# Moving ten of sixteen layernorm applications from VectorE to ScalarE, and rearranging the first ten microseconds of a fused attention and gated-MLP kernel

## The chip, the cores and the metric

The kernel runs on one core of one Trainium2 chip. The metric is device time in microseconds, lower is better. The profile of one execution comes with its own span, which is some 1.7 to 2.0 us shorter than the time on the metric, because it goes from the first to the last instruction.

Names used below: TensorE is PE in the profile, its weight loads are PEld, VectorE is DVE, ScalarE is ACT, GpSimd is POOL. SP is the engine that issues most DMAs; SPq and ACTq are the rows of DMA issues of SP and of ScalarE. PSUM is the memory that TensorE writes its results to; this kernel divides it into eight banks.

## The reference, cut to what matters

```python
x = A_x                                   # 1 x 2048 x 640, bf16
xn = layernorm(x)                         # (x - mean) / sqrt(var + 1e-5), per token
# branch A: 32 heads of 20, window of 8 positions at dilation 2
q, k, v = split(xn @ wqkv)
logits[s, w] = q[s] . k[s - 2*w] * 20**-0.5      # masked before the start
attn = softmax(logits, over w);  o[s] = sum_w attn[s, w] * v[s - 2*w]
# branch B: bilinear MLP, 640 -> 1536 -> 640
h = (xn @ w_gate) * (xn @ w_up)
out = x + o @ wo + h @ w_down
```

Of the kernel before, what the change touches and what calls it, by code (L numbers as in the profile page):

```python
# [5 lines left out]
ACT = mybir.ActivationFunctionType  # L6
ALU = mybir.AluOpType
# [3 lines left out]
NCH = 5  # L11
# [13 lines left out]
DHALF = D // 2  # L25
# [23 lines left out]
class Sched:  # L49
# [76 lines left out]
    def op(self, eng, fn, r=(), w=(), dma=False, name="", occ=None, lat=None, lock=False, nbytes=0, mode=0, group=None, extra=0.0):  # L126
        X = _Op()
        X.eng, X.fn, X.name, X.dma, X.group = eng, fn, name, dma, group
        X.needs_tick, X.event, X.pre_know, X.idx = False, None, None, len(self.ops)
        X.nth = self.n_eng[eng]  # L130
        self.n_eng[eng] += 1
        rk = [k for a in r for k in self.keys(a)]
        wk = [k for a in w for k in self.keys(a)]
        deps = self.deps_of(eng, rk, wk)
        if occ is None and not dma:
            occ = 0.1
        inorder = eng in ("pe", "act", "dve")
        start = max([self.t[eng]] + [d.end for d in deps.values()])
        if lock:
            start = max(start, self.t_lock)  # L140
        if eng == "pe" and mode != self.pe_mode:
            start += 0.1
            self.pe_mode = mode
        if dma:
            self.t[eng] = start + (0.48 if occ is None else occ)
            self.t_data = max(self.t_data, start + 1.2) + nbytes / 280e3
            X.end = self.t_data + 0.8 + extra
        else:
            self.t[eng] = start + occ
            X.end = start + (occ if lat is None else lat)  # L150
        if lock:
            self.t_lock = start + occ
        last = {}
        keep = []
        for d in deps.values():
            if d.dma or d.eng == "pool":
                keep.append(d)
            else:
                b = last.get(d.eng)
                if b is None or b.idx < d.idx:  # L160
                    last[d.eng] = d
        X.deps = keep + list(last.values())
        for d in X.deps:
            if not d.dma:
                d.needs_tick = True
        for k in rk:
            st = self.state.get(k)
            if st is None:
                self.state[k] = [None, [X]]
            elif inorder and st[1] and st[1][-1].eng == eng and not st[1][-1].dma:  # L170
                st[1][-1] = X
            else:
                st[1].append(X)
        for k in wk:
            self.state[k] = [X, []]
        if dma:
            if group is None or group not in self.groups:
                sem = self.nc.alloc_semaphore(f"dma{self.n_dma}")
                self.n_dma += 1
                if group is not None:  # L180
                    self.groups[group] = [sem, []]
            if group is None:
                X.event = (sem, 16)
            else:
                g = self.groups[group]
                g[1].append(X)
                X.event = (g[0], 16)
        self.ops.append(X)
        return X
# [151 lines left out]
def build_kernel(nc, A_x, A_wqkv, A_wo, B_x, B_w_gate, B_w_up, B_w_down, out):  # L341
    K = Sched(nc)
    op = K.op
# [3 lines left out]
    def sb(name, shape, dtype=BF16, at=None):  # L347
        n = mybir.dt.size(dtype)
        for s in shape[1:]:
            n *= s  # L350
        n = (n + 63) // 64 * 64
        if at is None:
            at = place[0]
            place[0] += n
        assert at + n <= 229344, (name, at + n)
        return K.sbuf(name, shape, dtype, at)
# [53 lines left out]
    MV = sb("MV", [128, NT, 16], FP32)  # L410
    SD = sb("SD", [128, NT, 16], FP32)
    DUM = sb("DUM", [128, 16], FP32)
    ZERO = sb("ZERO", [128, JB])
    EPSC = sb("EPSC", [128, 16], FP32)
    IDENT = sb("IDENT", [128, 128])
# [2 lines left out]
    PS = nc.alloc_psum_tensor("PS", [128, 8, 512], FP32)  # L418
# [8 lines left out]
    def mark(*k):  # L427
        done.add(k)
# [4 lines left out]
    def have(*k):  # L433
        return lambda: k in done
# [7 lines left out]
    def dma(o, i, r=(), w=(), name="", eng="sp", group=None):  # L442
        n = mybir.dt.size(o.dtype)
        for s in o.shape:
            n *= s
        return op(eng, lambda e: e.dma_start(o, i), r=r, w=w, dma=True, name=name, nbytes=n, group=group)  # L446

    op("dve", lambda e: e.memset(ZERO[:], 0.0), w=[ZERO[:]], name="zero", occ=0.2)
    op("dve", lambda e: e.memset(EPSC[:], EPS), w=[EPSC[:]], name="epsc", occ=0.1)
# [3 lines left out]
       r=[IDENT[:]], w=[IDENT[:]], name="ident", occ=0.4)  # L453
# [3 lines left out]
       r=[G[:]], w=[G[:]], name="g1", occ=0.3)  # L457
    op("pool", lambda e: e.affine_select(G[:], G[:], pattern=[[-4, H]], compare_op=ALU.is_ge,
                                         fill=0.0, base=0, channel_multiplier=1),
       r=[G[:]], w=[G[:]], name="g2", occ=0.3)  # L460
    op("pool", lambda e: e.memset(KT[:, :, 0:PAD], 0.0), w=[KT[:, :, 0:PAD]], name="kpad", occ=0.3)

    def xslot(t):
        return t + 4 if t < 8 else t - 8

    def x_load(t, eng="sp"):
        dma(XST[:, xslot(t), :], xhbm[t * TS:(t + 1) * TS, :], w=[XST[:, xslot(t), :]], name=f"xld{t}", eng=eng)
        mark("x", t)
# [44 lines left out]
    def front(t):  # L513
        x, st = XST[:, xslot(t), :], STATS[:, t, 0:12]
        xs, mv = XNS[:, t % NXN, :], MV[:, t, 0:2]
        sd, rstd = SD[:, t, 0:1], SD[:, t, 1:2]
        p = 0.1 * t

        def stats():
            for i in range(2):  # L520
                o, a = st[:, 6 * i:6 * i + 6], x[:, i * DHALF:(i + 1) * DHALF]
                op("dve", (lambda o, a: lambda e: e.bn_stats(o, a))(o, a), r=[a], w=[("st", t, i)], name=f"bn{t}_{i}", occ=0.49)  # L522

        def aggr():
            op("dve", lambda e: e.bn_aggr(mv, st), r=[("st", t, 0), ("st", t, 1)], w=[("mv", t)], name=f"bnag{t}", occ=0.2)

        def sqrt():
            op("act", lambda e: e.activation(sd, mv[:, 1:2], ACT.Sqrt, bias=EPSC[:, 0:1]), r=[("mv", t), EPSC[:]],
               w=[("sd", t)], name=f"sd{t}", occ=0.25)

        def apply():
            op("dve", lambda e: e.reciprocal(rstd, sd), r=[("sd", t)], w=[("rstd", t)], name=f"rstd{t}", occ=0.16)
            op("dve", lambda e: e.tensor_scalar(xs, x, mv[:, 0:1], rstd, op0=ALU.subtract, op1=ALU.mult),
               r=[x, ("mv", t), ("rstd", t)], w=[xs], name=f"lnap{t}", occ=0.45)
            mark("apply", t)

        yield have("x", t)
        yield Task("dve", stats, r=[x], prio=p)
        yield Task("dve", aggr, r=[("st", t, 1)], prio=p)
        yield Task("act", sqrt, r=[("mv", t)], prio=p)  # L540
        if t >= NXN:
            yield have("xnt", t - NXN)
        yield Task("dve", apply, r=[("sd", t), x], w=[xs], prio=p)
        o = XNT[:, :, t * TS:(t + 1) * TS]
        if t < N_PE_T:
            hold = []

            def trans(b):
                tpv = PS[:, b, :].bitcast(BF16)[:, 0:NCH * 128].rearrange("p (c f) -> p c f", c=NCH)
                for c in range(NCH):  # L550
                    i, q = xs[:, c * 128:(c + 1) * 128], tpv[:, c, :]
                    op("pe", (lambda q, i: lambda e: e.transpose(q, i, IDENT[:]))(q, i), r=[i, IDENT[:]], w=[q],  # L552
                       name=f"tr{t}_{c}", occ=0.057, lat=0.2)
                hold.append((b, tpv))
                if t == 0:
                    warm(3)

            def copy():
                b, tpv = hold[0]
                X = op("dve", lambda e: e.tensor_copy(o, tpv), r=[tpv], w=[o], name=f"xntcp{t}", occ=0.49)  # L560
                K.free_bank(b, X)

            yield Task("pe", trans, r=[xs], prio=p, banks=1)
            yield Task("dve", copy, r=[PS[:, hold[0][0], :]], prio=p)
        else:
            def dmat():
                op("sp", lambda e: e.dma_start_transpose(o, xs), r=[xs], w=[o], dma=True, name=f"dtr{t}", nbytes=200e3, occ=1.25, extra=1.3)

            yield Task("sp", dmat, r=[xs], prio=1)
        mark("xnt", t)  # L570

    def warm(n):
        for _ in range(n):
            op("pe", lambda e: e.matmul(PS[:, 7, 0:QB], ZERO[:, 0:128], ZERO[:, 0:QB], start=True, stop=True),
               r=[ZERO[:]], w=[PS[:, 7, :]], name="warm", occ=0.2 if n > 3 else 0.12)

# [422 lines left out]
    stores = []  # L999
# [53 lines left out]
                K.spawn(fin_thread())  # L1053

    N_PE_T = 5
    FIRST = 9
    GU_KEEP = 3

    x_load(0)
    x_load(1)  # L1060
    wqkv_load(0, 0, 3)
    wqkv_load(0, 3, NCH)
# [1 line left out]
    wqkv_load(1)  # L1064
    x_load(3)
    K.t["act"] = 2.1
    warm(22)

    def misc():
        yield have("xnt", NT - 1)  # L1070
# [65 lines left out]
```

## The kernel before: the parts that the change and the argument touch

The kernel is a program that makes a program. Each piece of work is a `Task` with an engine, the data it waits for, and a priority (a smaller number goes first). At build time a list scheduler with its own table of costs picks, per engine, among the tasks that it thinks are ready, and so fixes one order of instructions for each engine. On the chip each engine then works through its list in that order; if the next instruction has to wait, what stands behind it waits too.

The front, once for each of 16 tiles of 128 tokens (`...` marks cuts):

```python
def front(t):
    ...
    p = 0.1 * t
    def apply():
        op("dve", lambda e: e.reciprocal(rstd, sd), ...)
        op("dve", lambda e: e.tensor_scalar(xs, x, mv[:, 0:1], rstd, op0=ALU.subtract, op1=ALU.mult), ...)
    yield have("x", t)
    yield Task("dve", stats, r=[x], prio=p)          # two bn_stats of 320 columns
    yield Task("dve", aggr, r=[st], prio=p)
    yield Task("act", sqrt, r=[mv], prio=p)
    yield Task("dve", apply, r=[sd, x], w=[xs], prio=p)
    ...                                              # transposed on TensorE (tiles 0 to 4) or by DMA, into XNT
...
x_load(0); x_load(1); wqkv_load(0, 0, 3); wqkv_load(0, 3, NCH); x_load(2); wqkv_load(1); x_load(3)
warm(22)                                             # 22 dummy matmuls, to raise TensorE's clock
```

After the front come the projections to Q, K and V. Products of Q and K (tile PRD) are made on VectorE and summed to logits on TensorE. The softmax is done in two halves of 1024 tokens, nearly all on VectorE. V makes a detour: it is evicted to VST, stored to DRAM scratch in four parts of 512 tokens, and read back with shifted rows as VX. This detour and the copies of the softmax's result share one DMA queue:

```python
def store_v(j):                                       # one part of V: 640 KB
    yield num(NCH, "v", j)                            # its five evictions are done
    def go():
        dma(dst, VST[:, j], ..., name=f"vst{j}")      # on the SP queue
    yield Task("sp", go, r=[VST[:, j]], prio=20)

# in softmax(x): the weights move to another layout, 16 DMAs of 32 KB in one task
def move():
    for a in range(4):
        for q in range(4):
            ...
            dma(d, src, ..., name=f"atx{x}_{a}{q}")   # ATX <- LOG, also on the SP queue
yield Task("sp", move, r=[L[:]], prio=4)

# in vx_loads(): only when every logits block has been issued (num(NJ, "lg")), 4 DMAs a unit
yield have("vst", j)
yield Task("sp", go, prio=8, r=[("vscr", j)])         # VX <- v_scratch
```

While the attention goes on, TensorE fills its time with the gate and up projections of the MLP, each a group of five matmuls of 512 columns that needs one bank.

## Time and profile before

| | before |
|---|---|
| time, median of 3 runs (range) | 272.57 us (272.36 to 272.59) |
| span of the profiled run | 270.8 us |
| TensorE busy, share of the span | 265.4 us, 98% |
| VectorE busy, share of the span | 224.9 us, 83% |

The page of the kernel before starts with its span and with the busy time of every engine (share of the span, then number of instructions):

```profile
span 270.8 us, 4489 instructions
...
PE 265.4 (98%) x1811; PEld 153.6 (57%) x1811; DVE 224.9 (83%) x286; ACT 93.2 (34%) x169; POOL 96.5 (36%) x57
...
PE 89%; DVE 5%; DMA 3%; issue 1%; SPq 1%; ACT 0%; DVEq 0%
```

TensorE is the bottleneck: only 5.4 us of the span are without a matmul. The last line is the page's part 4, the chain of work that ended last, divided by engine.

The table of windows gives busy time and number of instructions of each engine in a stretch. These are the end of the front, the stretch in which tiles 6 to 15 are normalised, and the stretch around the second softmax, all of the kernel before:

```profile
core 0: us, PE busy (x) PEld busy (x) DVE busy (x) ACT busy (x) POOL busy (x), PEclk, DMA share, GB/s
6.72:10.84 4.12, 3.19 (x51) 2.85 (x51) 2.77 (x10) 1.65 (x4) 0.00 (x0) 1.00 1.02 352
20.00:33.00 13.00, 13.00 (x107) 11.24 (x106) 10.33 (x34) 8.55 (x21) 0.00 (x0) 1.00 0.52 87
96.00:112.50 16.50, 16.39 (x105) 7.17 (x104) 15.12 (x16) 8.07 (x12) 3.26 (x1) 1.00 0.82 210
```

In the first stretch TensorE is idle for 0.93 of 4.12 us. In the second it is never idle, and in the third hardly, for 0.11 us.

TensorE's timeline of the front, kernel before (start, duration, what; in brackets how long it was idle before, and who ended that):

```profile
1.26 4.59 PE L574 MATMUL PS<-ZERO 128*128 128x256 bf16 x22 [1.26 <-DVE EPSC L449]
5.69 0.44 PE L552 MATMUL PS<-IDENT,XNS 128*128 128x128 bf16 x5
...
9.03 1.31 PE L590 MATMUL PS<-XNT,WQKV 128*128 128x128 bf16 x20 [0.72 <-DVE XNT L560]
...
10.84 1.37 PE L590 MATMUL PS<-XNT,WQKV 128*128 128x128 bf16 x21 [0.22 <-DMA WQKV<-in_A_wqkv_dram]
```

These are the 22 dummies, the transposes of tile 0, the first four chunks of Q of tile 1, and K of tile 0, which waited for the second third of the projection weights.

### The profile page before, as it was taken

What the parts mean: (1) busy time and instruction counts of PE and PEld (TensorE: products, weight loads), DVE (VectorE), ACT (ScalarE), POOL (GpSimd) and SP (SyncE); (2) the same over time, 40 slices, a digit from 0 to 9 for tenths busy, and PEclk for the clock granted to TensorE, in tenths of its full rate; (3) what the DMA queues carried; (4) which work ended last, traced back from release to release, by engine and by line L of the source; (5) the groups of instructions that cost most, each with busy time, mean ns of one, the idle gap of its engine ahead of it and who ended that gap; (6) DMA issues with size and microseconds to landing.
All of it is one profiled execution on the core that took longest, in us unless ns stands there. A gap on an engine that the chain in (4) does not pass through costs nothing.

```text
span 270.8 us, 4489 instructions
## 1 busy us (share of the span) xinstructions
PE 265.4 (98%) x1811; PEld 153.6 (57%) x1811; DVE 224.9 (83%) x286; ACT 93.2 (34%) x169; POOL 96.5 (36%) x57
## 2 busy tenths in 40 slices
PE   7899999999999999999999999999999999999995
PEld 5897965454444444444444577544676776444775
DVE  5777799999999989999999999889989998623221
ACT  2466676555753245222433400433201202242000
POOL 1000000000000004077756876677857996600000
PEclk9999999999999999999999999999999999999999
DMA  6965459702343999127723356633364531100101
GB/s 202 361 207 83 92 81 322 264 0 97 99 130 78 240 207 319 39 49 163 177 69 80 105 130 166 185 83 79 79 174 132 138 88 48 48 2 0 48 27 48
DMA packets 39571, 33.46 MB, mean 124 GB/s; under 512 B 15232, under 2 KB 38272, under 8 KB 39552
## 3 DMA queue, kind: packets, MB, share of 16 engines
q1 hardware_dynamic: 39408, 33.15, 45.7%
q8 instruction: 14, 0.23, 0.4%
q10 hardware_dynamic: 144, 0.04, 0.1%
q14 instruction: 5, 0.04, 0.1%
HBM read 25.07 MB, written 5.26 MB: 112 GB/s over the span
## 4 chain that ended last, share of the span: by engine, by line
PE 89%; DVE 5%; DMA 3%; issue 1%; SPq 1%; ACT 0%; DVEq 0%
PE PS L966 33%; PE PS L1024 27%; PE PS L590 23%; DMA WQKV<-in_A_wqkv_dram 3%; PE PS L733 3%; PE PS L925 2%; DVE SM L762 2%; DVE PV L879 1%; SPq L446 1%; DVE HT L975 1%; DVE RS L782 1%; DVE M L762 0%; DVE LOG L773 0%; ACT PS L864 0%; PE PS L552 0%
## 5 line engine op out<-in xcount | busy, mean ns | idle before, releaser
L884 POOL TENSOR_TENSOR SV<-PV 128x1024 bf16<-128x1024 f32 x40 | 94.8, 2380 | 86.9 <-DVE PV L879 86.7
L879 DVE TENSOR_TENSOR PV<-VX,PS 128x1024 f32<-128x1024 bf16 (+1 forms) x56 | 92.9, 1670 | 1.7 <-ACT PS L864 1.7
L590 PE MATMUL PS<-XNT,WQKV 128*128 128x512 bf16 (+2 forms) x480 | 66.7, 299 | 1.2 <-DVE XNT L560 1.0
L966 PE MATMUL PS<-XNT,WG 128*128 128x512 bf16 x240 | 59.7, 379 | 0.1
L966 PE MATMUL PS<-XNT,WU 128*128 128x512 bf16 x240 | 59.7, 379 | 0.0
L590 PEld LDWEIGHTS PS<-XNT,WQKV 128*128 128x128 bf16 x480 | 43.4, 113 | 24.0 <-DVE XNT L560 1.7
L715 DVE TENSOR_TENSOR PRD<-QT,KT 128x2048 bf16<-128x2048 bf16 x40 | 46.1, 1218 | 0.0
L1024 PE MATMUL PS<-WD,HT 128*128 128x320 bf16 (+1 forms) x300 | 43.2, 294 | 0.0
L966 PEld LDWEIGHTS PS<-XNT,WU 128*128 128x128 bf16 x240 | 23.2, 98 | 29.1 <-ACT HT L595 0.8
L966 PEld LDWEIGHTS PS<-XNT,WG 128*128 128x128 bf16 x240 | 23.3, 98 | 28.6 <-DVE HT L975 0.6
L595 ACT ACTIVATE HT<-PS 128x512 bf16<-128x512 f32 x36 | 21.5, 597 | 51.6 <-PE PS L966 51.6
L1024 PEld LDWEIGHTS PS<-WD,HT 128*128 128x128 bf16 x300 | 28.6, 98 | 11.6 <-issue 0.4
L975 DVE TENSOR_TENSOR HT<-HT,PS 128x512 bf16<-128x512 bf16 x36 | 23.9, 683 | 12.7 <-PE PS L966 12.7
L1035 DVE TENSOR_TENSOR FOUT<-PS,XR 128x320 bf16<-128x320 f32 (+1 forms) x33 | 15.8, 478 | 16.9 <-PE PS L1024 16.5
L1024 PE MATMUL PS<-WO,OT 128*128 128x320 bf16 (+1 forms) x165 | 27.1, 295 | 0.0
L934 ACT ACTIVATE OT<-PS 128x512 bf16<-128x512 f32 x20 | 10.5, 600 | 36.8 <-PE PS L925 36.8
L1024 PEld LDWEIGHTS PS<-WO,OT 128*128 128x128 bf16 x165 | 15.9, 98 | 5.9
L752 POOL MEMSET LOG<- 32x6 bf16 (+6 forms) x7 | 0.4, 95 | 51.5 <-ACT LOG L744 51.5
L595 ACT ACTIVATE QT<-PS 128x512 bf16<-128x512 f32 (+1 forms) x22 | 12.3, 558 | 9.6 <-PE PS L590 9.5
L522 DVE BATCH_NORM_STATS2 STATS<-XST 128x6 f32<-128x320 bf16 x32 | 13.9, 476 | 2.0 <-DMA XST<-in_A_x_dram 1.9
L595 ACT ACTIVATE KT<-PS 128x512 bf16<-128x512 f32 (+1 forms) x22 | 12.2, 556 | 8.1 <-PE PS L590 8.1
L595 ACT ACTIVATE VST<-PS 128x512 bf16<-128x512 f32 x20 | 11.7, 597 | 8.1 <-PE PS L590 8.1
(43 smaller groups left out, 128.3 us busy)
## 6 DMA issues: line engine op xcount, KB each, us to landing
VX<-v_scratch SPq DMA_DIRECT2D x80, 130.0 KB, 2.9
XST<-in_A_x_dram SPq DMA_DIRECT2D x16, 160.0 KB, 7.1
v_scratch<-VST SPq DMA_DIRECT2D x4, 640.0 KB, 4.1
XR<-in_A_x_dram SPq DMA_DIRECT2D x16, 160.0 KB, 2.9
out_dram<-FOUT SPq DMA_DIRECT2D x15, 160.0 KB, 2.4
WG<-in_B_w_gate_dram SPq DMA_DIRECT2D x1, 1920.0 KB, 8.4
WU<-in_B_w_up_dram SPq DMA_DIRECT2D x1, 1920.0 KB, 12.0
WD<-in_B_w_down_dram SPq DMA_DIRECT2D x1, 1920.0 KB, 8.9
```

The lines of the kernel that those rows point to most:

```text
L522: op("dve", (lambda o, a: lambda e: e.bn_stats(o, a))(o, a), r=[a], w=[("st", t, i)], name=f"bn{t}_{i}", occ=0.49)
L590: op("pe", (lambda o, l, x, c, first: lambda e: e.matmul(o, l, x, start=first, stop=(c == NCH - 1)))(o, l, x, c, first), r=[l, x], w=[o], ...
L595: X = op("act", (lambda o, i: lambda e: e.activation(o, i, ACT.Copy))(o, i), r=[i], w=[o], name=name, occ=0.12 + n * 0.9e-3)
L715: op("dve", lambda e: e.tensor_tensor(s[:], qb, kv, ALU.mult), r=[q, rk], w=[s[:]], name=f"prod{j}_{r}_{c}", occ=1.15, lock=True)
L733: op("pe", (lambda o, x, a, c: lambda e: e.matmul(o, G[:], x, start=(c == 0), stop=(c == NCH - 1), tile_position=(0, 32 * a)))(o, x, a, c) ...
L879: op("dve", lambda e: e.tensor_tensor(p, vw, a, ALU.mult), r=[vv] + rk, w=[p], name=f"pv{u}_{x}_{r0}", occ=0.09 + 1.1 * nr)
L884: X = op("pool", lambda e: e.tensor_tensor(o, p[:, :, 0, :], p[:, :, 1, :], ALU.add), r=[p[:]], w=[o], name=f"pva{u}_{x}", occ=2.36, lock= ...
L934: X = op("act", (lambda o, b: lambda e: e.activation(o, PS[:, b, :], ACT.Copy))(o, b), r=[PS[:, b, :]], w=[o], name=f"oev{u}", occ=0.58)
L966: op("pe", (lambda l, x, c: lambda e: e.matmul(PS[:, b, :], l, x, start=(c == 0), stop=(c == NCH - 1)))(l, x, c), r=[l, x], w=[PS[:, b, :] ...
L975: X = op("dve", lambda e: e.tensor_tensor(h, h, PS[:, hold[1], :], ALU.mult), r=[h, PS[:, hold[1], :]], w=[h], name=f"h{m}_{j}", occ=0.65)
L1024: op("pe", (lambda l, x, i: lambda e: e.matmul(dst, l, x, start=(i == 0), stop=(i == n - 1)))(l, x, i), r=[l, x], w=[PS[:, b, :]], name=f" ...
L1035: X = op("dve", lambda e: e.tensor_tensor(o, PS[:, b, 0:wid], xr, ALU.add), r=[PS[:, b, :], xr], w=[o], name=f"fin{t}_{nb}", occ=0.15 + wi ...
```

## The change

It wants to shorten the front and to relieve VectorE: the first statistics of tile 1 go into VectorE's wait for tile 0's square root; a small read touches the weights' memory early; 18 dummies take the place of 22; and the normalisation of tiles 6 to 15 is done by ScalarE, as rstd * x - mean * rstd. One more thing happens that no line of the diff says: with these costs and priorities the scheduler puts five matmuls of Q (the fifth chunk of tiles 0 and 1) ahead of K. A setting `N_DVE_C = 5` has no effect, as only tiles 0 to 4 are copied there, so it is cut here.

```diff
+    TCH = sb("TCH", [128, 32])
 ...
+        def recip():
+            op("dve", lambda e: e.reciprocal(rstd, sd), ...)
+            if t >= N_DVE_A:
+                op("dve", lambda e: e.tensor_scalar(nmr, mv[:, 0:1], rstd, -1.0, op0=ALU.mult, op1=ALU.mult), ..., occ=0.13)
         def apply():
-            op("dve", lambda e: e.reciprocal(rstd, sd), ...)
-            op("dve", lambda e: e.tensor_scalar(xs, x, mv[:, 0:1], rstd, op0=ALU.subtract, op1=ALU.mult), ..., occ=0.45)
+            if t < N_DVE_A:
+                op("dve", lambda e: e.tensor_scalar(xs, x, mv[:, 0:1], rstd, op0=ALU.subtract, op1=ALU.mult), ..., occ=0.45)
+            else:
+                op("act", lambda e: e.activation(xs, x, ACT.Identity, bias=nmr, scale=rstd), ..., occ=0.75)
 ...
-        yield Task("dve", stats, r=[x], prio=p)
+        if t == 1:
+            yield have("sd", 0)
+        for i in range(2):
+            yield Task("dve", lambda: stats(i), r=[x], prio=-1 if t == 1 and i == 0 else p)
         yield Task("dve", aggr, r=[("st", t, 1)], prio=p)
-        yield Task("act", sqrt, r=[("mv", t)], prio=p)
+        yield Task("act", sqrt, r=[("mv", t)], prio=p - 1)
+        yield Task("dve", recip, r=[("sd", t)], prio=p)
 ...
-        yield Task("dve", apply, r=[("sd", t), x], w=[xs], prio=p)
+        yield Task("dve" if t < N_DVE_A else "act", apply, r=[("rstd", t), x], w=[xs], prio=p)
 ...
+    N_DVE_A = 6
 ...
     x_load(0)
+    tch = A_wqkv.rearrange("(p r) n -> p r n", r=NCH)[:, 0, 0:32]
+    stores.append(dma(TCH[:], tch, w=[TCH[:]], name="touch", eng="act"))
 ...
-    warm(22)
+    warm(18)
```

## The prediction

> **What bounds the kernel.** TensorE: the page gives PE 265.4 us busy of 270.8 (98%). The table of windows shows it busy 5.20 of 6.72 us before the first projection, 3.19 of 4.12 in 6.72-10.84, then at most 0.12 us idle in any stretch up to 229 us; after the last matmul come 2.7 us of eviction and store. From 10.84 us on the stream is dense, so a change in the front wins only what it starts earlier. Timeline of the front: x landed 3.1, statistics 3.12-4.01, square root to 4.57, normalised 5.26, last dummy 5.58, transposes 5.69, Q of tile 0 at 6.72, Q of tile 1 at 9.03 (PE idle 0.72 before it), K at 10.84, on the second weight third, landed 10.79.
>
> **The change, part by part.**
> 1. Fewer dummies: one starts every 0.213 us while the clock is low, so the row ends near 5.1. Tile 0's transposes start when it is normalised (about 5.4): up to 0.28 us earlier.
> 2. Tile 1's first statistics (0.44 us) in VectorE's 0.36 us wait for the square root: tile 0 loses 0.1, tile 1's Q starts at about 8.75 for 9.03.
> 3. The instruction order also moves Q's fifth chunk of tiles 0 and 1 (5 matmuls of 256 columns, 0.55 us) ahead of K, into the wait for the weights. This is the real gain: K starts at about 10.8 in both, with 0.55 us more done.
> 4. Touching read: DMA moves 113 and 159 GB/s in 3.0-4.0 us, against 330-380 later, just as weight reads begin. If the touch cures that, weights land up to 0.5 us earlier, but TensorE is busy until about 10.75 anyway: at most 0.1 us.
> 5. Ten normalisations to ScalarE: VectorE loses 10 x 0.45 us and gains ten one-column operations of about 0.13. ScalarE gains an estimated 0.9 us each: the square root of one column (0.29), plus 639 x 0.833 ns, plus 93 ns for a second pointer operand (the Trainium skill, "ScalarE: Activation LUTs", What ACT_TABLE_LOAD costs; the trace's 1.90 us for 2048 columns agrees with the slope). ScalarE, 67% busy in 16.7-31 us, becomes nearly full and falls an estimated 2 us behind TensorE; eight PSUM banks should carry this. VectorE starts the products some 3 us earlier, but no TensorE wait hangs on that.
>
> **Sum.** -0.6 us in the front, +0.1 for the chance of a bank wait in 20-36 us. Predicted 272.1 us, 8 times in 10 in 271.2 to 273.0. Chances: faster by over 2% 0.01, within 2% 0.97, slower by over 2% 0.02.
>
> **What would show it.** Timeline: transposes near 5.4, Q of tile 1 near 8.75, five 256-column matmuls before K, K at 10.5-10.9, no PE gap over 0.2 us later. Normalisation on ACT near 900 ns; ACT near 95% busy in 20-33 us; no PE wait on ACT. About 300 GB/s in 3.0-4.0 us if the touch works.
>
> **What would make it wrong.** TensorE's clock rose at about 5.4 us (dummies 213 ns apart before, 110 after). The Trainium skill, "TensorE: Matmul & The Clock Gate", What's actually happening, gives a busy window of about 3.4 us; 18 dummies end before the rise, and if it then comes later, the first projection (20 matmuls, 56 ns apart) takes about 1 us longer. ScalarE could delay evictions until TensorE waits for banks, +1 us or more. Weights that land much earlier could make the order pay more.

## More of the kernel before

The SP queue between 68 and 96 us, kernel before. The duration spans all DMA issues of a row:

```profile
70.64 4.55 SPq L446 DMA_DIRECT2D v_scratch<-VST  x2
75.68 10.46 SPq L446 DMA_DIRECT2D ATX<-LOG  x16
86.18 0.59 SPq L446 DMA_DIRECT2D v_scratch<-VST  x1
86.89 8.25 SPq L446 DMA_DIRECT2D VX<-v_scratch  x16
```

Three of the four V stores are issued before the 16 copies of the attention weights (the first of them at 61.66), one after. Those 16 copies are small, but their issuing alone takes 10.46 us. The third store was issued at 74.83 and had landed at 78.52; the fourth landed at 91.77.

VectorE in the stretch around the second softmax, kernel before:

```profile
97.14 2.35 DVE L879 TENSOR_TENSOR PV<-VX,PS 128x1024 f32<-128x1024 bf16 x2 [1.16 <-ACT PS L864]
...
100.12 0.75 DVE L762 TENSOR_TENSOR M<-M 128x512 bf16<-128x512 bf16 x2
...
102.05 1.28 DVE L975 TENSOR_TENSOR HT<-HT,PS 128x512 bf16<-128x512 bf16 x2
...
111.78 3.07 DVE L975 TENSOR_TENSOR HT<-HT,PS 128x512 bf16<-128x512 bf16 x5
```

The first products with V (PV) come here; then the second softmax (M are steps of its maximum); between 103.3 and 111.8 us VectorE makes no product of the MLP and so frees no bank. TensorE's groups in the same stretch:

```profile
98.18 1.25 PE L966 MATMUL PS<-XNT,WU 128*128 128x512 bf16 x5
...
111.14 1.24 PE L966 MATMUL PS<-XNT,WU 128*128 128x512 bf16 x5
112.52 1.25 PE L966 MATMUL PS<-XNT,WG 128*128 128x512 bf16 x5
```

After the logits block, from 98.18 us on, thirteen groups follow each other every 1.08 us. The thirteenth ends at 112.38. The fourteenth starts at 112.52, just after the first of the five HT products ended at 111.78 + 0.69 = 112.47. So VectorE was in time here with nothing to spare. The chain of waits of the kernel before says the same; these are the first and the last of its pieces there (start, duration, what):

```profile
97.14 2.35 DVE PV L879 x2
...
111.78 0.69 DVE HT L975
```

The chain runs through VectorE from 97.14 to 112.47 us.

ScalarE evicts a gate group to HT; VectorE multiplies an up group into it and so frees its bank:

```python
def mul():                                            # HT <- HT * PS
    X = op("dve", lambda e: e.tensor_tensor(h, h, PS[:, hold[1], :], ALU.mult), ...)
    K.free_bank(hold[1], X)
yield Task("dve", mul, r=[h, PS[:, hold[1], :]], prio=15)     # the softmax's steps have prio=10
```

## The result, and the profile after

| | before | after |
|---|---|---|
| time, median of 6 runs (range) | 272.47 us (272.08 to 272.59) | 273.11 us (272.83 to 273.65) |
| span of the profiled run | 270.8 us | 271.4 us |

The ratio is 1.0027, with a 95% interval of 1.0014 to 1.0040. Ratios here and below are the mean time of one kernel's fast runs over the mean of the other's in the same rounds, so they are not quite the ratio of the medians. The change made the kernel slightly slower: within 2%, but the interval excludes a gain, and the median lies above the predicted range.

The page of the kernel after, with the same lines as before:

```profile
span 271.4 us, 4493 instructions
...
PE 265.3 (98%) x1807; PEld 153.3 (56%) x1807; DVE 223.3 (82%) x286; ACT 100.2 (37%) x179; POOL 96.5 (36%) x57
...
PE 98%; DVE 1%; issue 0%; DVEq 0%
```

Read alone, it tells nothing of a loss: TensorE is still at 98%, and the chain of waits now hardly touches VectorE. The windows of the same three stretches, kernel after:

```profile
6.72:10.84 4.12, 3.53 (x58) 3.31 (x57) 2.73 (x8) 1.87 (x5) 0.00 (x0) 1.00 1.07 372
20.00:33.00 13.00, 13.00 (x102) 10.72 (x101) 11.05 (x42) 12.57 (x27) 0.00 (x0) 1.00 0.50 96
96.00:112.50 16.50, 15.00 (x70) 6.67 (x69) 16.26 (x19) 5.59 (x9) 3.33 (x2) 1.00 0.90 220
```

The front gained 0.34 us in the first stretch. In the second, ScalarE is now 97% busy (12.57 of 13.00) and TensorE still waits for nothing. The loss is in the third: TensorE is idle for 1.50 us there, and was for 0.11.

TensorE's timeline of the front, kernel after:

```profile
...
5.25 0.71 PE L566 MATMUL PS<-IDENT,XNS 128*128 128x128 bf16 x5
...
8.73 1.86 PE L607 MATMUL PS<-XNT,WQKV 128*128 128x128 bf16 x25 [0.59 <-DVE XNT L575]
10.70 1.50 PE L607 MATMUL PS<-XNT,WQKV 128*128 128x128 bf16 x24
```

The transposes start 0.44 us earlier and Q of tile 1 starts 0.30 us earlier. That row holds 25 matmuls instead of 20, the five of the fifth chunk, and K starts at 10.70 instead of 10.84. So the front is ahead by 0.14 us and by those five matmuls, which take 1.86 - 1.31 = 0.55 us: 0.69 us in all.

The new wait, in TensorE's timeline, kernel after:

```profile
93.17 1.25 PE L983 MATMUL PS<-XNT,WU 128*128 128x512 bf16 x5
...
106.14 1.24 PE L983 MATMUL PS<-XNT,WU 128*128 128x512 bf16 x5
108.88 1.25 PE L983 MATMUL PS<-XNT,WG 128*128 128x512 bf16 x5 [1.50 <-DVE HT L992]
```

Again thirteen groups, from 93.17 on, end at 107.38. Then TensorE has no bank, and waits 1.50 us for VectorE's HT product. The SP queue, kernel after:

```profile
68.75 0.37 SPq L447 DMA_DIRECT2D v_scratch<-VST  x1
72.13 11.41 SPq L447 DMA_DIRECT2D ATX<-LOG  x16
83.59 1.16 SPq L447 DMA_DIRECT2D v_scratch<-VST  x2
84.86 9.43 SPq L447 DMA_DIRECT2D VX<-v_scratch  x16
```

The copies of the attention weights start 3.55 us earlier (72.13 for 75.68), because VectorE reached the end of the first softmax earlier. But now two V stores stand behind them instead of one. They were issued at 83.59 and 84.22, and landed at 87.89 and 92.21. The four reads of VX's first unit landed at 92.32, 92.55, 92.81 and 93.42. In the kernel before they had landed between 91.89 and 92.99. So in absolute time VX is only 0.43 us later; it is late against the rest of the work, which has moved up by some 5 us (TensorE's thirteen groups start at 93.17 for 98.18). VectorE, kernel after:

```profile
93.50 2.35 DVE L896 TENSOR_TENSOR PV<-VX,PS 128x1024 f32<-128x1024 bf16 x2 [2.81 <-DMA VX<-v_scratch]
...
108.14 3.07 DVE L992 TENSOR_TENSOR HT<-HT,PS 128x512 bf16<-128x512 bf16 x5
```

VectorE sat idle for 2.81 us before the first PV, waiting for VX. Everything that follows is the same as before, in the same order and at the same pace: from the first PV to the first of the five HT products it is 108.14 - 93.50 = 14.64 us, and before it was 111.78 - 97.14 = 14.64 us. What changed is how the two engines stand to each other. Before, the first PV started 98.18 - 97.14 = 1.04 us ahead of TensorE's thirteen groups; now it starts 93.50 - 93.17 = 0.33 us behind them. That is 1.37 us, and the gap before the fourteenth group grew by 1.50 - 0.14 = 1.36 us. The sum is -0.69 + 1.36 = +0.67 us; measured were +0.64 us.

### The profile page after: what moved, and what is told of

Its sections match the earlier page's. It is cut to its first block, busy times and chain, and to the rows that moved or that the text cites. A ratio compares the mean times of both kernels' runs of the same rounds, so it can differ in the third digit from the quotient of the medians.

```text
span 271.4 us, 4493 instructions
## 1 busy us (share of the span) xinstructions
PE 265.3 (98%) x1807; PEld 153.3 (56%) x1807; DVE 223.3 (82%) x286; ACT 100.2 (37%) x179; POOL 96.5 (36%) x57
## 4 chain that ended last, share of the span: by engine, by line
PE 98%; DVE 1%; issue 0%; DVEq 0%
PE PS L983 38%; PE PS L1041 27%; PE PS L607 24%; PE PS L750 3%; PE PS L942 2%; PE PS L591 2%; PE PS L566 1%; DVE HT L992 0%; DVE XNT L575 0%; DVE FOUT L1052 0%; DVE ZERO L449 0%; DVEq L319 0%; DVE EPSC L450 0%
## 5 line engine op out<-in xcount | busy, mean ns | idle before, releaser
L522 DVE BATCH_NORM_STATS2 STATS<-XST 128x6 f32<-128x320 bf16 x32 | 14.7, 469 | 1.8 <-DMA XST<-in_A_x_dram 1.8
L1041 PE MATMUL PS<-WD,HX 128*128 128x320 bf16 x96 | 14.4, 299 | 0.0
```

What stands on the lines that cost most here:

```text
L522: op("dve", lambda e: e.bn_stats(o, a), r=[a], w=[("st", t, i)], name=f"bn{t}_{i}", occ=0.49)
L1041: op("pe", (lambda l, x, i: lambda e: e.matmul(dst, l, x, start=(i == 0), stop=(i == n - 1)))(l, x, i), r=[l, x], w=[PS[:, b, :]], name=f" ...
```

## The experiments

The theory from the traces: the front gained what was predicted, and the ScalarE part lost more, through the order of the DMA queue. V's third store went behind the 16 copies, VX came late, VectorE came late to its HT products, and TensorE ran out of banks. There were four rivals or additions: ScalarE, nearly full in 20 to 33 us, does the harm itself; the clock rises too late with 18 dummies; the touching read disturbs or helps the weights; and VX's lateness is innocent, the order on VectorE alone being at fault. Each batch of kernels ran on one chip together with the kernel before, and medians are compared within the batch. The kernel before had 272.57, 272.61, 272.74 and 272.73 us in the four batches. All results were correct.

| kernel | median us (range) | n | ratio to before | 95% interval |
|---|---|---|---|---|
| e1 front only | 272.03 (271.85 to 272.34) | 5 | 0.9981 | 0.9968 to 0.9994 |
| e2 ScalarE part only | 277.33 (276.82 to 278.08) | 4 | 1.0178 | 1.0160 to 1.0195 |
| e3 after, two V stores on ScalarE's queue | 272.05 (271.77 to 272.55) | 5 | 0.9986 | 0.9972 to 0.9999 |
| e4 after, HT products first | 271.84 (271.29 to 273.14) | 6 | 0.9983 | 0.9964 to 1.0002 |
| e5 e4 without touch | 271.99 (271.44 to 272.27) | 6 | 0.9978 | 0.9965 to 0.9991 |
| e6 e4 with 22 dummies | 272.63 (271.68 to 273.57) | 6 | 1.0002 | 0.9984 to 1.0020 |
| e7 e4, fifth chunk held back | 273.98 (273.63 to 275.27) | 6 | 1.0059 | 1.0041 to 1.0077 |
| e8 before, HT products first | 272.25 (271.93 to 272.49) | 5 | 0.9987 | 0.9975 to 1.0000 |
| e9 e2, HT products first | 273.06 (272.13 to 273.30) | 6 | 1.0009 | 0.9994 to 1.0025 |
| e10 e4 and e3 together | 271.62 (271.49 to 273.53) | 6 | 0.9976 | 0.9954 to 0.9998 |
| e11 e10 without touch | 271.73 (271.58 to 271.89) | 5 | 0.9968 | 0.9956 to 0.9981 |
| e12 e1, HT products first | 271.83 (271.53 to 272.34) | 6 | 0.9975 | 0.9962 to 0.9987 |
| e13 e1, fifth chunk held back | 272.69 (272.56 to 273.08) | 5 | 1.0006 | 0.9990 to 1.0021 |
| e14 e1 with 22 dummies | 272.29 (272.05 to 272.62) | 5 | 0.9988 | 0.9973 to 1.0002 |
| e15 e1 without the early statistics | 272.40 (272.14 to 272.64) | 5 | 0.9993 | 0.9979 to 1.0006 |

### e1 and e2: each half of the change alone

e1 is the kernel after with all normalisations back on VectorE:

```diff
-    N_DVE_A = 6
+    N_DVE_A = 16
```

> The change without its ScalarE normalisation (all 16 tiles on VectorE); the issue order then stores three of the four V parts ahead of the attention-weight copies, as before. Theory (front won 0.7 us; the late V store cost 1.4): 271.8 us, PE gap before the gate matmuls near 107-112 us at most 0.2 us, first VX landing before the weights' copies are done. Rival (the loss lies in the front itself, by the later rise of TensorE's clock): still about 273.1, no better than the whole change.

e2 is the kernel before with only the ScalarE part:

```diff
+            if t >= N_DVE_A:
+                op("dve", lambda e: e.tensor_scalar(nmr, mv[:, 0:1], rstd, -1.0, ...), ...)
-            op("dve", lambda e: e.tensor_scalar(xs, x, mv[:, 0:1], rstd, ...), ...)
+            (t < N_DVE_A: the same on VectorE; otherwise:)
+                op("act", lambda e: e.activation(xs, x, ACT.Identity, bias=nmr, scale=rstd), ...)
+    N_DVE_A = 6
```

> The kernel before with only the ten normalisations on ScalarE. Theory: no front gain, two V stores behind the sixteen attention-weight copies, VectorE waits 2 to 3 us for VX near 90 us, TensorE stalls about 1.4 us: 273.9 us. Rival (ScalarE's load, evictions late in 20-36 us): PE gaps in 20-40 us instead, and no gap near 107.

The front alone is 0.54 us faster than before (medians). In e1 the SP queue has three V stores before the 16 copies, as the kernel before has, PV waits for nothing but ScalarE's copy (1.44 us), and TensorE has no gap over 0.2 us around the second softmax. The front's gain is as predicted.

The ScalarE part alone is 4.76 us slower. The direction was expected, the size was not. This is TensorE's timeline of e2, and two windows of it:

```profile
106.03 1.24 PE L976 MATMUL PS<-XNT,WG 128*128 128x512 bf16 x5
110.11 2.19 PE L976 MATMUL PS<-XNT,WU 128*128 128x512 bf16 x5 [2.84 <-DVE HT L985]
112.09 2.04 PE L976 MATMUL PS<-XNT,WG 128*128 128x512 bf16 x5
```

```profile
106.00:110.10 4.10, 1.27 (x6) 0.39 (x4) 4.03 (x5) 0.60 (x1) 0.72 (x1) 1.00 1.12 220
110.10:113.40 3.30, 3.29 (x9) 1.20 (x10) 3.30 (x5) 0.00 (x0) 0.00 (x0) 0.53 0.93 207
```

There is a gap of 2.84 us at the same place (and one of 0.60 us at 101.1, before the group that starts at 101.70). Then the group that takes 1.24 us at full clock takes 2.19 us: the granted clock is 0.53 for 3.3 us. At about half rate that costs an estimated 1.6 us more (3.3 us at 0.53). In three of the four runs the mean granted clock was 0.993 or 0.994; the one at 1.0 was the fastest, with 276.82 us, so most of the 4.76 us are not the clock. It was faster than the next by only 0.41 us, which is less than the estimate; that run has no trace, and why stays open. The two halves do not add up to the whole (-0.54 and +4.76 against +0.64), because each build has an order of its own.

Why the gap is larger here than in the kernel after can be read from VectorE's timeline of e2:

```profile
97.00 2.78 DVE L772 TENSOR_TENSOR M<-M 128x512 bf16<-128x512 bf16 x2
...
109.43 0.63 DVE L985 TENSOR_TENSOR HT<-HT,PS 128x512 bf16<-128x512 bf16 x1
```

Two V stores stand behind the copies in e2 too, and the first PV waits 2.00 us for VX. But from the first PV, at 92.89, to this HT product it is 16.54 us, where it is 14.64 us in the kernels before and after. The two steps of the maximum take 2.78 us, against 0.75 us in the kernel before, while GpSimd works on SV (96.45 to 99.18 us). The kernels before and after show the same once: a step of the softmax's sum takes 2.72 us in the second softmax, beside GpSimd's first SV, and 0.69 us in the first softmax, where GpSimd is idle. So GpSimd's work seems to lengthen VectorE's second softmax by some 2 us in the kernels before and after, and by some 4 us in e2, where both steps are long. This is an inference from the overlap in time; no run tests it. If it is right, the overlap takes more than the 1.50 us that TensorE waits in the kernel after, and moving GpSimd's work might be a third cure.

### e3: take the V stores out of the queue behind the copies

```diff
-            dma(dst, VST[:, j], ..., name=f"vst{j}")
+            dma(dst, VST[:, j], ..., name=f"vst{j}", eng="act" if j >= 2 else "sp")
-        yield Task("sp", go, r=[VST[:, j]], prio=20)
+        yield Task("act" if j >= 2 else "sp", go, r=[VST[:, j]], prio=20)
```

> The whole change, with V stores 2 and 3 issued from ScalarE's queue, so that they need not stand behind the copies on SyncE's. Theory: VX lands about 87-90 us, VectorE's wait of 2.8 us goes, TensorE's stall falls from 1.5 to at most 0.2 us: 271.7 us. Rival (the stall comes from VectorE's softmax being too early against TensorE's groups, whatever VX does): stall stays over 1 us, 273.1.

The first of the two V stores in the timeline of ScalarE's DMA issues, and then VectorE's timeline, both of e3:

```profile
74.24 0.38 ACTq L447 DMA_DIRECT2D v_scratch<-VST  x1
...
```

```profile
92.22 2.35 DVE L896 TENSOR_TENSOR PV<-VX,PS 128x1024 f32<-128x1024 bf16 x2 [1.44 <-ACT PS L881]
...
106.86 3.07 DVE L992 TENSOR_TENSOR HT<-HT,PS 128x512 bf16<-128x512 bf16 x5
```

The third V store goes out at 74.24 and has landed at 78.38 (the fourth at 82.02 and 87.82): its data were there, and in the kernel after it stood behind the issuing of the copies until 83.59. VX's first unit has landed at 89.55 instead of 93.42. VectorE's wait for it is gone; what it waits for now is the same copy by ScalarE as before the change. The five HT products start at 106.86, some 13.6 us after TensorE's first group began (the trace has four of its five matmuls, from 93.50 on, so it began near 93.28; kernel after: 14.97 us, kernel before: 13.60 us), and no gap over 0.2 us is left. The time is 0.52 us below that of the kernel before. ScalarE had all its ten normalisations in this kernel, so the rival that its load does the harm is refuted: the harm went away with the V stores' place in the queue.

The Trainium skill, "DMA: Bandwidth & Descriptors", Issuing engines are not separate DMA queues, says that issuing from several engines only saves the sequencer's time, "which is usually small relative to the DMA itself". The trace agrees that it is issue time that is saved, and differs on its size: 16 copies of 32 KB occupied the issuing queue for 11.41 us, and a store of 640 KB, which takes 4.1 us from issue to landing in e3 and 3.7 us in the kernel before, stood behind them for some 9 us (74.24 to 83.59).

### e4: leave VX late, but let VectorE free the banks first

```diff
-                yield Task("dve", mul, r=[h, PS[:, hold[1], :]], prio=15)
+                yield Task("dve", mul, r=[h, PS[:, hold[1], :]], prio=9)
```

> The whole change, with VectorE's gate products put ahead of the second softmax in its order; VX lands as late as in the change. Theory (TensorE stalls because its PSUM banks wait for those products behind the softmax): no gap over 0.3 us near 107 us though VectorE still waits over 2 us for VX: about 271.7 us. Rival (TensorE waits for data that VX delays, not for banks): stall stays, 273.1.

VectorE in e4:

```profile
93.27 2.35 DVE L896 TENSOR_TENSOR PV<-VX,PS 128x1024 f32<-128x1024 bf16 x2 [2.82 <-DMA VX<-v_scratch]
95.54 0.68 DVE L992 TENSOR_TENSOR HT<-HT,PS 128x512 bf16<-128x512 bf16 x1
...
103.91 0.67 DVE L992 TENSOR_TENSOR HT<-HT,PS 128x512 bf16<-128x512 bf16 x1
```

VX is as late as in the kernel after (2.82 us of waiting), yet TensorE's gap is gone, because the HT products now stand between the softmax's steps. The median is 0.73 us below that of the kernel before, though the interval just reaches 1. So the late VX by itself costs nothing that these runs can show. The loss needs both: VX late, and a VectorE program that frees no bank for the length of the second softmax. Mending either one is enough.

### e8, e9: the same priority without the front

e8 and e9 are the kernel before and e2, each with the one-line edit of e4.

> The kernel before, with gate products first on VectorE. Theory (before had only 0.12 us of stall there): 272.3 to 272.6, unchanged. Rival (the gain of e4 has nothing to do with the change, it would come to any kernel): 271.8 or less.

> e2 (only the ten normalisations on ScalarE) with gate products first on VectorE. Theory (all of e2's loss is the stall behind the softmax, and the clock that falls in it): no PE gap over 0.6 us after 20 us, granted clock 1.0 in all runs, 272.2 to 272.8 us. Rival (ScalarE's normalisation costs by itself): 274 or more.

e8 is about as fast as the kernel before, possibly 0.1% faster. e9 takes away nearly all of e2's loss, though it is a small miss: its median of 273.06 us lies above the expected 272.2 to 272.8. This is the same stretch in e9, in the table of windows:

```profile
96.00:112.50 16.50, 16.50 (x79) 7.42 (x77) 16.43 (x17) 6.21 (x9) 10.87 (x5) 1.00 1.11 265
```

TensorE is busy all the time there, at full clock. So both parts of e2's 4.8 us, the waits and the half clock after them, hung on the order of VectorE's program, and the ScalarE part in itself gives about nothing: e9's median is 0.32 us above that of the kernel before, with 1 inside the interval. The build moved more than the HT products, though: the sum of the second softmax starts at 122.9 us in e9, and at 103.3 in e2.

### e5, e6, e7: the front's pieces, in the version with HT first

e5 takes the touching read out of e4, e6 has `warm(22)` instead of `warm(18)`, and e7 holds the fifth chunk of Q back until K of tile 0 is done:

```diff
-    stores.append(dma(TCH[:], tch, w=[TCH[:]], name="touch", eng="act"))     (e5)
-    warm(18)
+    warm(22)                                                                 (e6)
-                K.spawn(proj_group([(which, 4, 1)], pair * TS, 2 * TS, 10.2, None))
+                K.spawn(fifth(which, pair))       (e7: the same, after num(2, "qk", 1, 0, 0) for the first pair)
```

> Gate products first (as e4), without the touching read; the issue order is otherwise the same. Theory (the touch buys nothing, TensorE has other work until the second weight third lands): within 0.2 us of e4's 271.8. If the touch works: second weight third lands about 0.5 to 1 us later than with it and K of tile 0 waits for it, 272.1 or more. If the touch hurts (weights 0 land later with it): 271.5.

> Gate products first (as e4), with 22 dummies again. Theory (fewer dummies win the start of the transposes, 0.3 to 0.4 us, but pay with a clock that rises after them): equal within 0.2 us, 271.8. If fewer dummies help: 272.1. If they hurt by the late clock: 271.5.

> Gate products first (as e4), with Q's fifth chunk of tiles 0 and 1 held back until K of both tiles is evicted, as in the kernel before. Theory: K waits for the weights with TensorE idle; if the second weight third lands at 9.75 to 10.4 us (with the touch), the idle time is at most 0.5 us: 272.0 to 272.3 us, 0.2 to 0.5 above e4. Rival (the moved chunk is worth nothing): equal to e4.

e5: taking the touching read away changes nothing that can be seen. With it, the second third of the weights landed between 9.75 and 10.60 us in eleven profiled kernels; without it, between 10.01 and 10.79 in six. The medians of the two sets are 10.19 and 10.27, which is little beside a spread of 0.8 us in each.

e6 is inconclusive: its runs spread over 1.9 us, its median is above all that was expected (271.5 to 272.1), and its interval overlaps those of e4 and e5.

e7 is a miss. It was expected at 272.0 to 272.3 us and took 273.98. Its trace shows why it can't serve: the build changed the later order too, with gaps of 0.34 us at 10.77, 0.58 us at 104.7 and 0.24 us at 118.8. In the profiled run TensorE's clock also rose only at 7.3 us. An experiment in this kernel has to be looked at for what else it moved.

### e10, e11, e12: the best that comes out of it

e10 has the edits of e3 and e4 together, e11 is e10 without the touching read, and e12 is e1 (no ScalarE part) with the edit of e4.

> The whole change with both cures: gate products first, and V stores 2 and 3 from ScalarE's queue. Theory: the stall is gone with either, so both give no more than one: 271.6 to 272.0 us. Rival (each cure takes only a part): 271.3 or less.

> e10 without the touching read: a second pair for what the touch is worth. Theory (nothing): within 0.2 us of e10. If the touch helps: 0.3 us or more slower.

> The front part alone (e1, all normalisations on VectorE) with gate products first. Theory (e1 had no stall, so the new order adds nothing and ScalarE's normalisation earns nothing): 271.8 to 272.1 us, equal to e1 and e10 within 0.3. Rival (moving the normalisation to ScalarE pays once the stall is gone): slower than e10 by 0.4 or more.

e11 has the lowest ratio, 0.9968: it beats the kernel before by 0.3% and the kernel after by some 0.6%, the latter worked out from two ratios of different batches (0.9968 / 1.0027 = 0.994). But e1, e4, e5, e10, e11 and e12 can't be told apart by their intervals. e12 gets 0.9975 with all normalisations on VectorE. So moving them to ScalarE has earned nothing that these runs can show, even with its damage mended.

### e13, e14, e15: which piece of the front pays

These start from e1, where the later order is like that of the kernel before. e13 holds the fifth chunk back as e7 does, e14 has 22 dummies, and e15 has no early statistics:

```diff
-        if t == 1:
-            yield have("sd", 0)
-            yield Task("dve", lambda: stats(i), r=[x], prio=-1 if t == 1 and i == 0 else p)
+            yield Task("dve", lambda: stats(i), r=[x], prio=p)               (e15)
```

> e1 (front only, no stall) with Q's fifth chunk held back until K of tiles 0 and 1 is evicted; TensorE's later order is then that of the kernel before. Cleaner than e7, whose later order changed too. Theory (the moved chunk is most of the front's gain): 272.3 to 272.6, equal to before within 0.2 us. Rival (dummies, early statistics and touch are the gain): equal to e1, 0.5 below before.

> e1 with 22 dummies again; no other change of order. Theory (fewer dummies matter little): 0.4 to 0.6 us below before, as e1. Rival (they are the gain): equal to before.

> e1 with tile 1's first statistics after tile 0's normalisation again; the fifth chunk stays ahead of K, one V chunk moves. Theory (tile 1's Q starts 0.3 us later, then the stream is dense): 0.2 to 0.4 us below before. Rival (worth nothing): as e1.

e13 is as fast as the kernel before (272.69 against 272.73 us), although its front is the new one in all else. Its timeline of TensorE:

```profile
8.59 1.31 PE L607 MATMUL PS<-XNT,WQKV 128*128 128x128 bf16 x20 [0.59 <-DVE XNT L575]
...
10.64 2.04 PE L607 MATMUL PS<-XNT,WQKV 128*128 128x128 bf16 x33
```

Q of tile 1 is 0.44 us earlier than in the kernel before, but without the fifth chunk there is nothing to do in the time won, and K starts only 0.20 us earlier. So it is the moved chunk that pays; the intervals of e1 and e13 overlap a little (0.9990 to 0.9994), and the traces agree with this reading. e14 and e15 lie between e1 and the kernel before, and their intervals overlap both. Their ratios lie 0.0007 and 0.0012 above that of e1, which would be 0.2 and 0.3 us for the dummies and the early statistics; these runs do not establish either.

## Why the prediction was right or wrong

Predicted were 272.1 us, in a range of 271.2 to 273.0; the measured median is 273.11 us. The class, within 2%, was right; the direction and the range were wrong.

- Fewer dummies and early statistics: the transposes were predicted near 5.4 and came at 5.25 us; Q of tile 1 at 8.75, and it came at 8.73. Right.
- The fifth chunk ahead of K as "the real gain": right, and e13 supports it. The front's "-0.6 us" is e1's -0.54 us.
- The touching read: predicted as worth at most 0.1 us, and shown by about 300 GB/s in 3.0 to 4.0 us "if the touch works". It did not: the window had 136 GB/s before and 133 after. e5 shows no effect.
- ScalarE's cost: predicted 0.9 us each, from the Trainium skill, "ScalarE: Activation LUTs", What ACT_TABLE_LOAD costs (93 ns for each pointer operand, 0.833 ns per element). The trace agrees, with 920 ns. ScalarE was predicted near 95% busy in 20 to 33 us and was at 97%, and TensorE did not wait for it. The new one-column operation on VectorE was estimated at 130 ns and takes 214 ns; that was harmless. These are the two groups in the kernel after (the first from the lines by form: count, then busy us and mean ns, then idle us before it; the second from the view of tile XNS, with the shortest, median and longest of ten in ns):

```profile
L535 DVE TENSOR_SCALAR SD<-MV,SD 128x1 f32<-128x1 f32 x10 | 2.1, 214 | 0.4
...
L543 ACT ACTIVATE XNS<-XST,SD x10: 919/920/922, 20.3 to 35.0; 128x640 bf16<-128x640 bf16 x10
```

- The step that failed, in the prediction's words: "VectorE starts the products some 3 us earlier, but no TensorE wait hangs on that." VectorE did gain its 3 us: the products (PRD) started at 33.5 us for 36.5, and the copies after the first softmax started 3.55 us earlier. But two things hung on it. First, the order of the SP queue: copies that are ready earlier came ahead of a V store that had been ahead of them, and this held VX back until 93.4 us (e3 takes it away). Second, VectorE's second softmax stood ahead of the HT products that free TensorE's banks, and TensorE had no slack there (e4 takes that away). Together they are a wait of 1.50 us, where the prediction had put 0.1 us for a bank wait, and in the wrong place, "in 20-36 us".
- How it could have been seen beforehand: the prediction took "at most 0.12 us idle in any stretch up to 229 us" to mean that nothing but an earlier start can be won; it did not ask what could be lost there. The page of the kernel before gave VectorE 5% of the chain of waits, and the chain lists 97.14 to 112.47 us as its place. And the order is fixed at build time: the two traces show V's third store changing place with the 16 copies, so a comparison of the two built programs, which needs no chip, would have to show it too. The prediction looked at the instruction order for the fifth chunk and says nothing of the DMA queue.
- "What would make it wrong" named a late rise of the clock. In the profile of the kernel after, the clock did rise late: three dummies at 5.75, 5.97 and 6.18 us were still as far apart as on the low clock, so the rise came at 6.2 us or later, and the transposes, 107 ns apart for 56, took 0.71 us for 0.44. That costs that one run about 0.3 us at the transposes. By the spacing of the matmuls, the rise came anywhere from 4.4 to 7.3 us in the 17 profiled kernels: at about 4.4 in e2 and 5.4 in the kernel before, both with 22 dummies. All six kernels with 22 dummies had it by 5.5 us. Of the eleven with 18, four had it later: e11 at about 5.7, the kernel after at some 6.3, e10 at 7.1 and e7 at 7.3. One profile of each kernel can't settle whether the dummies do this: if they do not, the four late ones still fall among those eleven about one time in seven. The Trainium skill, "TensorE: Matmul & The Clock Gate", What's actually happening, calls the window free-running and so the point of transition variable; the traces agree. A late rise did not make the loss: e1, e3, e4, e5, e10 and e11, all with 18 dummies, ended below the kernel before, and so did the very run of e10 (271.96 us) whose clock rose at 7.1. Whether 18 or 22 is better was not resolved.

## What to carry to other kernels

Before you call an engine's relief harmless, look for stretches where the bottleneck is barely idle while the chain of waits runs through another engine: there is no slack there, and a reordering of a few microseconds becomes a stall. In a kernel whose order is fixed at build time, compare the whole built order, the DMA queues too, since a group of small DMAs that gets ready earlier may block a large and urgent one behind its issuing. Put work that frees a bottleneck's buffers ahead of longer work that only feeds a later stage; here that one priority repaired the loss, and without the ScalarE part the kernel was as fast.

## What the Trainium skill lacked or had wrong

- "DMA: Bandwidth & Descriptors", Issuing engines are not separate DMA queues: it calls the issue time on the sequencer "usually small relative to the DMA itself". Here 16 copies of 32 KB took 11.41 us to issue, some 0.7 us each, against a median of 1.9 us from issue to landing, and this delayed a 640 KB store by 9 us; moving two stores to ScalarE's queue turned a loss of 0.64 us into a gain of 0.52 us, each against the kernel before in its own batch.
- "TensorE: Matmul & The Clock Gate", HAM oscillation — how this bites in real kernels: its rule is no idle gaps over about 3.4 us. In the profiled run of e2 a gap of 2.84 us, with 1.27 us of work in the 4.10 us around it, was followed by 3.3 us at a granted clock of 0.53, and two more of its four runs have the same low mean clock. So a gap shorter than the page names can be followed by a lower clock; the fourth run stayed at 1.0, and as it has no trace, its gaps are not known. The 1.50 us of the kernel after were not followed by one.
- "TensorE: Matmul & The Clock Gate", What's actually happening: it puts the variation of the transition at 500 ns either way. Here the clock rose between 4.4 and 7.3 us after the first instruction, in kernels that all began their dummies at 1.26 us; that is a spread of 2.9 us, against 1.0 us on the page. TensorE has pauses of up to 0.7 us among these matmuls, so the cases are not quite alike.
- No page says what an early small read of a weight's memory does for the reads that follow. Here it did nothing that could be seen: 136 GB/s without it and 133 with it, between 3.0 and 4.0 us.
